# Decode attention with cached keys in SBUF: one slot of transposed K parked in two PSUM banks, a third V slot kept in SBUF

## The chip, the cores and the metric

The kernel runs on one NeuronCore of a Trainium2 chip. The metric is the device time of one execution in microseconds. Before the change it is 1142.0 us, the median of three runs (1141.01 to 1142.94). The profile shown was taken from one more execution of the same kernel, which took 1143.57 us; its span from the first to the last instruction is 1141.8 us.

## The reference

Two identical layers are applied one after the other to eight tokens (one per batch row). A layer is attention over a cache followed by a small dense block, each behind a layer norm without weights and a residual. Both layers read the same caches and the same weights.

```python
B, Sq, D = 8, 1, 512
Hq, Hkv, Sk, Dh = 32, 8, 8192, 128
# _A_ref(x, k_cache, v_cache, wq, wo):
q = (x @ wq).reshape(B, Sq, Hq, Dh).transpose(0, 2, 1, 3)
k = jnp.repeat(k_cache, 4, axis=1)
v = jnp.repeat(v_cache, 4, axis=1)
p = softmax(jnp.einsum("bhqd,bhkd->bhqk", q, k) * Dh ** -0.5)
o = jnp.einsum("bhqk,bhkd->bhqd", p, v)
... o (all heads) @ wo
# _B_ref(x, w1, w2):   silu(x @ w1) @ w2,  F = 1792
x = x + _A_ref(_layernorm(x), K, V, wq, wo)
x = x + _B_ref(_layernorm(x), w1, w2)
x = x + _A_ref(_layernorm(x), K, V, wq, wo)
x = x + _B_ref(_layernorm(x), w1, w2)
```

Everything is bfloat16. The two caches hold 134 MB each, far more than the on-chip memory, so most of them is read from HBM twice, once for each layer.

## The kernel before

**Tasks, chunks and slots.** A *task* is (layer, batch row b, K/V head g): 2 x 8 x 8 = 128 tasks. A task has four *chunks* k = 0..3 of 2048 cache rows. A chunk of K or of V is 512 KB and fills one of NSLOT = 28 *slots* of the SBUF tensor `arena`. Chunks are numbered c = 0..511 in the order of the tasks.

**What is done for a chunk.** The main loop (lines 946 to 987) runs over c. In iteration c it transposes K of chunk c on TensorE, eight 128x128 blocks into each of two PSUM banks (`emit_t`, line 520), ScalarE copies the first bank back over the first half of the slot (line 537) and VectorE the second (line 539); then `emit_pv` (line 608) multiplies the probabilities with V of chunk c-6 (LAG = 6), and `emit_s` (line 550) multiplies q with the transposed K of chunk c, into one of two score banks. Once per task come the row maximum (line 568), the exponential (line 581), the sums, and `emit_pt` (line 592), which transposes the probabilities P on TensorE into a bank of the same ring as K's transposes, from where VectorE copies them (line 601). This happens in iteration c = 4i+1 of the next task, between PV and the scores. A compute engine works strictly in the order in which the program emits its instructions.

**The ring.** The banks `TPp` are a ring of NTP = 3, counted by `evacs`: each half of a K chunk takes the next bank and each P transpose one more. PSUM has eight banks here: two for scores, `OTp` for the PV product, `UP`, three `TPp`, and `MISC` for the projections.

**What stays between the layers.** For each b the last KEEP = 20 of the 32 K chunks (heads 3 to 7) stay in SBUF, already transposed, from layer 0 to layer 1, and so do the last KEEPV = 2 V chunks. They are not loaded again in layer 1. `make_tasks` (line 137) orders the tasks so that for each b there is a run of five layer-0 tasks with g = 3..7 (I call it the *filling* run: each chunk loads K and V, K stays), then five or six tasks of other heads whose K and V stream through (the *streaming* run: 22 slots are held, six turn over), then five layer-1 tasks with g = 3..7 (the *emptying* run: no K load, no K transposes, V loads only, and each chunk gives a slot back).

**The loads.** `lay_loads` (line 193) writes the list of loads at build time. Positions are half-steps: 2c stands after PV of iteration c and 2c+1 after its scores. Every load has a position `need` at which it is used and a position `free` at which its slot is given back; it takes the slot that is free longest, and `after` is the position at which that slot was given back. Two loads of neighbouring chunks can be joined into one of 1 MB over two neighbouring slots (8 KB instead of 4 KB per partition, "wide"). SP issues all loads in the order of this list, each one behind a wait for the last reader of its slot. In the last three tasks K is transposed one chunk ahead (LEAD = 1, from chunk 500).

**The chain between the layers.** When a batch row has its eight layer-0 heads, `chain_of` (line 764) computes residual, layer norm, dense block, second norm and the new q in small steps put between the chunks. A projection of one token leaves its result in `MISC` in rows; `upright` (line 744) turns it with a VectorE 32x32-block transpose into `UP`, and the next operations read `UP`. There are five such turns for each b.

**Start.** The first AHEAD = 8 chunks of K are transposed, then `lay_runs` (line 489) brings eleven 512 KB runs of the weights into place through all eight PSUM banks, then q of layer 0 is projected when `wq` has landed.

Of the kernel before, what the change touches and what calls it, by code (L numbers as in the profile page):

```python
# [14 lines left out]
HALVES = 2  # L15
SPT = 4
NSLOT = 28
KEEP = 20
KEEPV = 2
LAG = 6  # L20
WIDE = 8
AHEAD = 8
LEAD = 1
NTP = 3
NSCP = 2
NQB = 2
NST = 4
KB = 512
# [141 lines left out]
    return 0 if (d.g, d.k) in kept else d.layer, d.b, d.g, d.k // 2  # L170


def plan_loads(tasks, kept, keptv, nslot, ngran):

    single = set()
    while True:
        loads = lay_loads(tasks, kept, keptv, nslot, ngran, single)
        double = {rows_of(d, kept) for d in loads if d.n == 2}
        torn = {rows_of(d, kept) for d in loads if d.n == 1} & double
        if not torn:  # L180
            return loads, double
        single |= torn


# [5 lines left out]
    return i * SPT  # L190


def lay_loads(tasks, kept, keptv, nslot, ngran, single):

    at = {t: i for i, t in enumerate(tasks)}
    wanted = []
    late = closing_from(tasks, kept)
    for i, (layer, b, g) in enumerate(tasks):
        for k in range(ngran):
            c = i * SPT + k  # L200
            if layer == 0 or (g, k) not in kept:
                last = i if layer or (g, k) not in kept else at[(1, b, g)]
                wanted.append(Load("K", layer, b, g, k, -1 if c < AHEAD else 2 * (c - LEAD if c >= late else c), 2 * (last * SPT + k) + 1))
            if layer == 0 or (g, k) not in keptv:
                last = i if layer or (g, k) not in keptv else at[(1, b, g)]
# [3 lines left out]
    loads = []  # L209
# [20 lines left out]
    return loads  # L230


def bass_interleave_layers__gqa_block_cached__dense_activation_silu__decode_kernel(
# [15 lines left out]
def _build(ctx, nc, A_x, A_k_cache, A_v_cache, A_wq, A_wo, B_w1, B_w2, out):  # L249
# [5 lines left out]
    KT = D // 128  # L255
# [12 lines left out]
    loads, wide = plan_loads(tasks, kept, keptv, NSLOT, NGRAN)  # L268
    NC = len(tasks) * SPT

    pe = nc.tensor
# [61 lines left out]
    last_use = [max(d.free for d in loads if d.slot <= s < d.slot + d.n) for s in range(NSLOT)]  # L333
    spare = last_use.index(min(last_use))

    def apart(space, shapes):
# [37 lines left out]
    def r_half(slot, h):  # L374
        return res(f"slot{slot}_{h}")
# [46 lines left out]
    with nc.Block() as block:  # L422

        @block.sync
        def _(sync_eng):
# [94 lines left out]
            def emit_t(c, h):  # L520
                if c >= NC:
                    return
                layer, b, g, k = where(c)
                if layer and (g, k) in kept:
                    return
                slot = k_slot[(b, g, k)]
                tb = evacs[0] % NTP
                evacs[0] += 1
                tpv = TPp[tb][:, :].rearrange("p (k q) -> p k q", q=128)
                steps = [  # L530
                    lambda c=c: pe.transpose(tpv[:, c, :], chunk(slot, h * GRP + c), ident[:, :])  # L531
                    for c in range(GRP)
                ]
                mm_group(steps, reads=[r_half(slot, h), "ident"], writes=[f"TP{tb}"])
                dst = half(slot, h)
                if h == 0:
                    op(act, lambda: act.copy(dst, TPp[tb][:, :]), reads=[f"TP{tb}"], writes=[r_half(slot, h)])  # L537
                else:
                    op(dve, lambda: dve.tensor_copy(dst, TPp[tb][:, :]), reads=[f"TP{tb}"], writes=[r_half(slot, h)])  # L539

            def emit_q(ti):
                layer, b, g = tasks[ti]
# [199 lines left out]
                return w.rearrange("p (c t b) -> p t c b", t=NT, b=QR)[:, :, c0:c1, :]  # L742

            def upright(n):
                op(dve, lambda: dve.transpose(UP[:, 0:n * QR], MISC[:, 0:n * QR]), reads=["MISC"], writes=["UP"])  # L745

            def sum_rows(xnew, rnew, xold, rold, by):
                upright(KT)
                op(dve, lambda: dve.scalar_tensor_tensor(
                    xnew, UP[:, 0:KT * QR:QR].unsqueeze(2), by, xold, op0=ALU.mult, op1=ALU.add),  # L750
                   reads=["UP", rold], writes=[rnew])

            def add_residual(xnew, rnew, xold, rold, n):
                op(
# [9 lines left out]
            def chain_of(b):  # L764
# [11 lines left out]
                hv = UP[:, 0:FT * QR:QR]  # L776

                def expo():
                    upright(FT)
                    op(act, lambda: act.activation(eh, hv, ACT.Tanh, scale=0.5), reads=["UP"], writes=["eh"])  # L780

                def silu():
                    op(dve, lambda: dve.scalar_tensor_tensor(hsT, eh, 1.0, hv, op0=ALU.add, op1=ALU.mult),
                       reads=["UP", "eh"], writes=["hsT"])

                def down(q0, q1):
                    def run():
# [12 lines left out]
                def answer(a):  # L800
                    def run():
                        upright(AC)
                        op(dve, lambda: dve.tensor_copy(qt2[:, a * AC:(a + 1) * AC], UP[:, 0:KB:QR]),
                           reads=["UP"], writes=[rq2])
                    return run

                n1, n2 = ln_stages(x1, "XT1", 1, one), ln_stages(x2, "XT2", 1, one)
# [138 lines left out]
            for c in range(NC + LAG):  # L946
# [81 lines left out]
```

## Time and profile before

| | |
|---|---|
| median of three runs | 1142.0 us |
| profiled execution | 1143.57 us, span 1141.8 us |
| TensorE busy | 937.2 us (82%), mean granted clock 0.917 |
| VectorE busy | 548.5 us (48%) |
| ScalarE busy | 482.9 us (42%) |
| DMA queue of SP | 456.71 MB, 99.3% of 16 engines |
| K and V loads | 283 of K and 363 of V, 202 of them 1 MB, the others 512 KB |

The profile is one execution. Its page gives busy times, the span in 40 slices, the DMA queues, and the chain of work that ended last (followed back from the last instruction to what released each step). Of the trace, groups of instructions, waits, stretches of time and single instructions can be asked for. Matmuls are pipelined, so a busy TensorE is not one at its peak. Times in the trace are in us from the start of the span, durations of single instructions are given in us or ns as marked.

### The profile page before, as it was taken

The page shows a single profiled execution, that of the slowest core. Times are in us where ns is not written, and L with a number is a line of the kernel's source. Part 1 is how long each engine was busy: PE and PEld are TensorE (multiplying, and loading weights), DVE is VectorE, ACT ScalarE, POOL GpSimd, SP SyncE. Part 2 cuts the span into 40 slices and gives each one's busy share as a digit, 9 for nine tenths or more (in the row PEclk, how much of TensorE's full clock was granted, in tenths as well). Part 3 has the DMA queues.
Part 4 walks back from the last instruction along what each step waited for, and adds up shares of the span by engine and source line. Part 5 has one row for each costly group of instructions (what it writes and reads, how often), then busy time and mean ns, then how long its engine had stood idle before and what let it go on. Part 6 is the DMA issues. An engine that isn't in the chain of part 4 may idle for free.

```text
span 1141.8 us, 42932 instructions
## 1 busy us (share of the span) xinstructions
PE 937.2 (82%) x18792; PEld 698.9 (61%) x18792; DVE 548.5 (48%) x1702; ACT 482.9 (42%) x770; POOL 117.4 (10%) x300
## 2 busy tenths in 40 slices
PE   7588888888888888888888887888788888888796
PEld 4366664666566665766566655666466655666565
DVE  7344553446434553446444553446444553446443
ACT  6254541554335441554235442554245432554332
POOL 0000101001110111001100011001100111001110
PEclk9698997999889996999889997999889997999887
DMA  9999999999999999999999999999999999999995
GB/s 378 413 414 414 395 403 413 419 411 397 412 418 417 394 404 419 419 405 396 414 418 415 392 404 418 418 401 398 413 417 403 391 395 420 417 389 392 396 420 225
DMA packets 96270, 459.45 MB, mean 402 GB/s; under 512 B 10700, under 2 KB 10964, under 8 KB 69716
## 3 DMA queue, kind: packets, MB, share of 16 engines
q1 hardware_dynamic: 96068, 456.71, 99.3%
q8 instruction: 148, 2.42, 0.9%
q14 instruction: 38, 0.31, 0.1%
q10 hardware_dynamic: 16, 0.01, 0.0%
HBM read 456.66 MB, written 0.01 MB: 400 GB/s over the span
## 4 chain that ended last, share of the span: by engine, by line
DMA 56%; PE 27%; DVE 9%; issue 4%; SPq 2%; ACT 0%; POOL 0%; POOLq 0%; ACTq 0%; DVEq 0%
DMA arena<-in_A_v_cache_dram 41%; PE TPp L531 14%; DMA arena<-in_A_k_cache_dram 12%; DVE arena L539 7%; PE SCp L557 6%; PE OTp L617 4%; DMA wq<-in_A_wq_dram 2%; PE MISC L732 2%; SPq L391 2%; PE TPp L597 1%; DVE small L606 0%; DVE small L587 0%; ACT P L581 0%; PE MISC L704 0%; DVE small L577 0%
## 5 line engine op out<-in xcount | busy, mean ns | idle before, releaser
L537 ACT COPY arena<-TPp 128x1024 bf16<-128x1024 bf16 x352 | 356.1, 1012 | 412.8 <-PE TPp L531 410.1
L539 DVE COPY arena<-TPp 128x1024 bf16<-128x1024 bf16 x352 | 243.4, 691 | 350.2 <-PE TPp L531 347.8
L531 PE MATMUL TPp<-ident,arena 128*128 128x128 bf16 x5632 | 389.4, 224 | 26.1 <-DMA arena<-in_A_k_cache_dram 23.4
L531 PEld LDWEIGHTS TPp<-ident,arena 128*128 128x128 bf16 x5632 | 328.2, 100 | 119.8 <-DMA arena<-in_A_k_cache_dram 66.8
L617 PE MATMUL OTp<-PT,arena 128*128 128x32 bf16 x8192 | 293.2, 179 | 74.2 <-DMA arena<-in_A_v_cache_dram 69.9
L617 PEld LDWEIGHTS OTp<-PT,arena 128*128 128x128 bf16 x8192 | 251.7, 98 | 159.6 <-DMA arena<-in_A_v_cache_dram 129.3
L557 PE MATMUL SCp<-arena,QB 128*32 128x512 bf16 x2048 | 223.8, 430 | 74.0 <-DVE arena L539 23.1
L581 ACT ACTIVATE P<-SCp,small 128x512 bf16<-128x512 f32 x128 | 87.9, 687 | 206.5 <-DVE small L579 139.8
L568 DVE TENSOR_REDUCE small<-SCp 128x1 f32<-128x512 f32 x128 | 88.5, 691 | 113.5 <-PE SCp L557 112.3
L557 PEld LDWEIGHTS SCp<-arena,QB 128*32 128x32 bf16 x2048 | 61.0, 96 | 115.2 <-ACT arena L537 62.1
L572 POOL PARTITION_ALL_REDUCE small<-small x128 | 47.5, 371 | 618.6 <-DVE small L570 618.6
L589 POOL PARTITION_ALL_REDUCE small<-small x128 | 55.2, 432 | 338.2 <-DVE at L631 155.1
L597 PE MATMUL TPp<-ident,P 128*128 128x128 bf16 x512 | 54.4, 235 | 9.6 <-ACT P L581 9.0
L587 DVE TENSOR_SCALAR small<-small 128x4 f32<-128x4 f32 x128 | 28.5, 223 | 37.9 <-ACT P L581 37.9
L601 DVE COPY PT<-TPp 128x256 bf16<-128x256 bf16 x128 | 36.6, 286 | 11.1 <-PE TPp L597 9.3
L597 PEld LDWEIGHTS TPp<-ident,P 128*128 128x128 bf16 x512 | 32.4, 102 | 12.8 <-ACT P L581 12.5
L570 DVE TENSOR_SCALAR small<-small 128x4 f32<-128x4 f32 x128 | 29.3, 229 | 4.5
L577 DVE TENSOR_TENSOR small<-small 128x4 f32<-128x4 f32 x128 | 19.9, 156 | 20.9 <-POOL small L572 20.9
L745 DVE STREAM_TRANSPOSE UP<-MISC 128x128 f32<-128x128 f32 (+2 forms) x40 | 22.1, 552 | 14.7 <-PE MISC L732 14.7
L732 PE MATMUL MISC<-wo,at 128*32 128x128 bf16 x1024 | 26.2, 232 | 0.0
L581 ACT ACTIVATION_READ_ACCUMULATOR P<-SCp,small 128x1 f32 x128 | 24.7, 193 | 0.0
L579 DVE TENSOR_REDUCE small<-small 128x1 f32<-128x4 f32 x128 | 20.1, 157 | 4.4
(96 smaller groups left out, 284.7 us busy)
## 6 DMA issues: line engine op xcount, KB each, us to landing
arena<-in_A_v_cache_dram SPq DMA_DIRECT2D x133, 1024.0 KB, 14.5
arena<-in_A_v_cache_dram SPq DMA_DIRECT2D x230, 512.0 KB, 6.6
arena<-in_A_k_cache_dram SPq DMA_DIRECT2D x214, 512.0 KB, 6.9
arena<-in_A_k_cache_dram SPq DMA_DIRECT2D x69, 1024.0 KB, 20.6
arena<-in_A_wo_dram SPq DMA_DIRECT2D x8, 512.0 KB, 13.9
wq<-in_A_wq_dram SPq DMA_DIRECT2D x1, 4096.0 KB, 25.1
w<-in_B_w_dram SPq DMA_DIRECT2D x1, 1792.0 KB, 22.3
arena<-in_B_w_dram SPq DMA_DIRECT2D x3, 512.0 KB, 17.1
```

The costliest lines, as they stand in the source:

```text
L531: lambda c=c: pe.transpose(tpv[:, c, :], chunk(slot, h * GRP + c), ident[:, :])
L537: op(act, lambda: act.copy(dst, TPp[tb][:, :]), reads=[f"TP{tb}"], writes=[r_half(slot, h)])
L539: op(dve, lambda: dve.tensor_copy(dst, TPp[tb][:, :]), reads=[f"TP{tb}"], writes=[r_half(slot, h)])
L557: lambda t=t: pe.matmul(SCp[bank][t * QR:(t + 1) * QR, :], QB[qn][:, NGRAN - 1 - k:NGRAN - 1 - k + QR], keys[:, t * KB:(t + 1) * KB], star ...
L568: op(dve, lambda: dve.tensor_reduce(mxp[st][:, :], SCp[bank][:, :], AX.X, ALU.max), reads=[f"SC{bank}"], writes=[f"mxp{st}"])
L572: op(pool, lambda: pool.partition_all_reduce(mxa[st][:, :], mxr[st][:, :], 128, bass.bass_isa.ReduceOp.max), reads=[f"mxr{st}"], writes=[f ...
L581: op(act, lambda: act.activation(P[:, :], SCp[bank][:, :], ACT.Exp, bias=nb[st][:, 0:1], scale=SM_SCALE, accum_out=rs[st][:, :]), reads=[f ...
L589: op(pool, lambda: pool.partition_all_reduce(ssa[st][:, :], ssm[st][:, :], 128, bass.bass_isa.ReduceOp.add), reads=[f"ssm{st}"], writes=[f ...
L597: lambda c=c: pe.transpose(tpv[:, c, :], P[:, c * 128:(c + 1) * 128], ident[:, :])
L601: op(dve, lambda: dve.tensor_copy(PT[:, :, :, :], tpv.rearrange("p c (t q) -> p c t q", q=QR)[:, :, :, 0:NGRAN * REP]), reads=[f"TP{tb}"], ...
L617: lambda n=n, cc=cc: pe.matmul(otp, chunk(slot, n), PT[:, cc % CPB, (cc // CPB) % NT, cc // (CPB * NT)::NGRAN].unsqueeze(2).to_broadcast([ ...
L732: lambda t=t, col=col, w=w, start=start, stop=stop: pe.matmul(MISC[t * QR:(t + 1) * QR, 0:math.prod(w.shape[1:])], spread(col), w, start=s ...
```

## The change

Three things change together.

1. *Parking.* Of the 20 kept K chunks of each b, the last one, (g, k) = (7, 3), no longer stays in SBUF. Its transposes of layer 0 go to two PSUM banks of their own, `KEPTp`, instead of ring banks. They are copied into the slot for the scores of layer 0 as before (`set_down`), then the slot is given back while the two banks keep their content. In layer 1, `emit_unpark` copies the two banks once more into a slot, by ScalarE and VectorE, one iteration before the scores need it. The slot comes from the planner, which picks the slot given back latest, but before position need - 1.
2. *A third V slot.* KEEPV goes from 2 to 3: V of (7, 1) now also stays between the layers and is not loaded in layer 1.
3. *The banks.* `UP` is dropped: VectorE turns `MISC` in place, and the operations that read `UP` read `MISC`. The ring of K's transposes goes from three banks to two. The weights at the start go through MISC in place of UP, and through the two ring and two KEPT banks.

```diff
-KEEPV = 2
+KEEPV = 3
+PARK = 1
...
-NTP = 3
+NTP = 2
...
-                last = i if layer or (g, k) not in kept else at[(1, b, g)]
+                last = i if layer or (g, k) not in kept - parked else at[(1, b, g)]
...
+            elif (g, k) in parked:
+                wanted.append(Load("C", layer, b, g, k, 2 * (c - 1), 2 * c + 1))
...
+        if d.kind == "C":
+            d.slot = max((j for j in range(nslot) if free[j] < d.need - 1), key=lambda j: (free[j], j))
+            free[d.slot] = d.free
+            copies.append(d)
+            continue
...
-    UP = ps_bank("UP")
     TPp = [ps_bank("TPp", BF16) for _ in range(NTP)]
     MISC = ps_bank("MISC")
+    assert PARK == 1
+    KEPTp = [ps_bank("KEPTp", BF16) for _ in range(HALVES)]
...
-                wide = [(SCp[0], "SC0"), (SCp[1], "SC1"), (OTp, "OT"), (UP, "UP")]
-                wide2 = [(TPp[n][:, :].bitcast(FP32), f"TP{n}") for n in range(NTP)] + [(MISC, "MISC")]
+                wide = [(SCp[0], "SC0"), (SCp[1], "SC1"), (OTp, "OT"), (MISC, "MISC")]
+                wide2 = [(p[n][:, :].bitcast(FP32), f"{r}{n}") for p, r in ((TPp, "TP"), (KEPTp, "KEPT")) for n in range(2)]
...
-                tb = evacs[0] % NTP
-                evacs[0] += 1
-                tpv = TPp[tb][:, :].rearrange("p (k q) -> p k q", q=128)
+                if (g, k) in parked:
+                    bank, rt = KEPTp[h], f"KEPT{h}"
+                else:
+                    tb = evacs[0] % NTP
+                    evacs[0] += 1
+                    bank, rt = TPp[tb], f"TP{tb}"
+                tpv = bank[:, :].rearrange("p (k q) -> p k q", q=128)
...
-                mm_group(steps, reads=[r_half(slot, h), "ident"], writes=[f"TP{tb}"])
+                mm_group(steps, reads=[r_half(slot, h), "ident"], writes=[rt])
+                set_down(bank, rt, slot, h)
+
+            def set_down(bank, rt, slot, h):
                 dst = half(slot, h)
                 if h == 0:
-                    op(act, lambda: act.copy(dst, TPp[tb][:, :]), reads=[f"TP{tb}"], writes=[r_half(slot, h)])
+                    op(act, lambda: act.copy(dst, bank[:, :]), reads=[rt], writes=[r_half(slot, h)])
                 else:
-                    op(dve, lambda: dve.tensor_copy(dst, TPp[tb][:, :]), reads=[f"TP{tb}"], writes=[r_half(slot, h)])
+                    op(dve, lambda: dve.tensor_copy(dst, bank[:, :]), reads=[rt], writes=[r_half(slot, h)])
+
+            def emit_unpark(d):
+                k_slot[(d.b, d.g, d.k)] = d.slot
+                for h in range(HALVES):
+                    set_down(KEPTp[h], f"KEPT{h}", d.slot, h)
...
-                op(dve, lambda: dve.transpose(UP[:, 0:n * QR], MISC[:, 0:n * QR]), reads=["MISC"], writes=["UP"])
+                op(dve, lambda: dve.transpose(MISC[:, 0:n * QR], MISC[:, 0:n * QR]), reads=["MISC"], writes=["MISC"])
...
-                        op(dve, lambda: dve.tensor_copy(qt2[:, a * AC:(a + 1) * AC], UP[:, 0:KB:QR]),
-                           reads=["UP"], writes=[rq2])
+                        op(dve, lambda: dve.tensor_copy(qt2[:, a * AC:(a + 1) * AC], MISC[:, 0:KB:QR]),
+                           reads=["MISC"], writes=[rq2])
...
                     emit_pv(c - LAG)
                     if (c - LAG) % SPT == SPT - 1:
                         emit_norm((c - LAG) // SPT)
+                while copies and copies[0].need <= 2 * c:
+                    emit_unpark(copies.pop(0))
                 issue_until(2 * c)
                 soft(c - SPT - 1, emit_pt)
```

More of the change, by code (lines that the diff above doesn't have):

```diff
@@ L170, in rows_of, with plan_loads @@
     return 0 if (d.g, d.k) in kept else d.layer, d.b, d.g, d.k // 2
-def plan_loads(tasks, kept, keptv, nslot, ngran):
+def plan_loads(tasks, kept, parked, keptv, nslot, ngran):
     single = set()
     while True:
-        loads = lay_loads(tasks, kept, keptv, nslot, ngran, single)
+        loads, copies = lay_loads(tasks, kept, parked, keptv, nslot, ngran, single)
         double = {rows_of(d, kept) for d in loads if d.n == 2}
@@ L180, in plan_loads @@
         if not torn:
-            return loads, double
+            return loads, copies, double
         single |= torn
@@ L190, in closing_from, with lay_loads @@
     return i * SPT
-def lay_loads(tasks, kept, keptv, nslot, ngran, single):
+def lay_loads(tasks, kept, parked, keptv, nslot, ngran, single):
     at = {t: i for i, t in enumerate(tasks)}
@@ L208, in lay_loads @@
     free = [-2] * nslot
-    loads = []
+    loads, copies = [], []
     while wanted:
         d = wanted.pop(0)
+        if d.kind == "C":
[3 more added lines that the diff above has]
+            continue
         mate = None
@@ L229, in lay_loads @@
         loads.append(d)
-    return loads
+    return loads, copies
 def bass_interleave_layers__gqa_block_cached__dense_activation_silu__decode_kernel(
@@ L267, in _build @@
     task_at = {t: i for i, t in enumerate(tasks)}
-    loads, wide = plan_loads(tasks, kept, keptv, NSLOT, NGRAN)
+    parked = set(order[len(order) - PARK:])
+    loads, copies, wide = plan_loads(tasks, kept, parked, keptv, NSLOT, NGRAN)
     NC = len(tasks) * SPT
@@ L332, in _build @@
     vr, yr, tr, s1, s1a = [few(B) for _ in range(5)]
-    last_use = [max(d.free for d in loads if d.slot <= s < d.slot + d.n) for s in range(NSLOT)]
+    last_use = [max(d.free for d in loads + copies if d.slot <= s < d.slot + d.n) for s in range(NSLOT)]
     spare = last_use.index(min(last_use))
@@ L749, in sum_rows @@
                 op(dve, lambda: dve.scalar_tensor_tensor(
-                    xnew, UP[:, 0:KT * QR:QR].unsqueeze(2), by, xold, op0=ALU.mult, op1=ALU.add),
-                   reads=["UP", rold], writes=[rnew])
+                    xnew, MISC[:, 0:KT * QR:QR].unsqueeze(2), by, xold, op0=ALU.mult, op1=ALU.add),
+                   reads=["MISC", rold], writes=[rnew])
             def add_residual(xnew, rnew, xold, rold, n):
@@ L774, in up @@
                            for k in range(KT) for t in range(NT)], ["w1", "xn1"])
-                hv = UP[:, 0:FT * QR:QR]
+                hv = MISC[:, 0:FT * QR:QR]
                 def expo():
                     upright(FT)
-                    op(act, lambda: act.activation(eh, hv, ACT.Tanh, scale=0.5), reads=["UP"], writes=["eh"])
+                    op(act, lambda: act.activation(eh, hv, ACT.Tanh, scale=0.5), reads=["MISC"], writes=["eh"])
                 def silu():
                     op(dve, lambda: dve.scalar_tensor_tensor(hsT, eh, 1.0, hv, op0=ALU.add, op1=ALU.mult),
-                       reads=["UP", "eh"], writes=["hsT"])
+                       reads=["MISC", "eh"], writes=["hsT"])
                 def down(q0, q1):
```

## The prediction

> **What bounds the kernel now.** I read the page first: the busy shares, the 40 slices with the DMA rows, the queue table and the head of the chain.
>
> ```profile
> span 1141.8 us, 42932 instructions
> PE 937.2 (82%) x18792; PEld 698.9 (61%) x18792; DVE 548.5 (48%) x1702; ACT 482.9 (42%) x770; POOL 117.4 (10%) x300
> ...
> DMA  9999999999999999999999999999999999999995
> GB/s 378 413 414 414 395 403 413 419 411 397 412 418 417 394 404 419 419 405 396 414 418 415 392 404 418 418 401 398 413 417 403 391 395 420 417 389 392 396 420 225
> ...
> q1 hardware_dynamic: 96068, 456.71, 99.3%
> ...
> DMA 56%; PE 27%; DVE 9%; issue 4%; SPq 2%; ACT 0%; POOL 0%; POOLq 0%; ACTq 0%; DVEq 0%
> ```
>
> The DMA engines are busy in every slice but the last; SP's queue alone takes 99.3% of them. TensorE, 82% by a modelled measure, is the largest share of the chain after DMA (27%). So the question is whether TensorE is ever the one that holds the end back. That needs the stretches. The next view gives busy times, clock, DMA share and rate for the end of one batch row's cycle: three tasks of an emptying run (from 303.3), its last task with the first filling one half begun (318.5), one filling task (338.8), two streaming tasks (384.9 and 395), and the time behind the last load.
>
> ```profile
> 303.30:308.80 5.50, 4.30 (x86) 2.55 (x84) 1.94 (x9) 0.86 (x3) 0.80 (x2) 0.81 1.02 424
> 308.80:313.90 5.10, 4.85 (x88) 2.72 (x84) 2.02 (x9) 0.87 (x3) 0.80 (x2) 0.50 1.01 422
> 313.90:318.50 4.60, 4.02 (x92) 2.55 (x88) 2.02 (x9) 0.86 (x3) 0.80 (x2) 0.97 1.01 413
> 318.50:328.60 10.10, 6.49 (x137) 4.44 (x136) 3.44 (x13) 2.66 (x6) 1.17 (x3) 0.79 1.01 417
> 338.80:347.90 9.10, 7.41 (x152) 6.13 (x152) 4.39 (x13) 4.92 (x7) 0.80 (x2) 1.00 1.01 419
> 384.90:395.00 10.10, 8.61 (x180) 6.49 (x180) 5.54 (x18) 4.92 (x7) 1.60 (x4) 1.00 0.99 377
> 395.00:405.70 10.70, 9.35 (x224) 7.27 (x224) 6.56 (x22) 5.21 (x9) 0.81 (x2) 1.00 1.01 401
> 1131.40:1139.30 7.90, 4.69 (x148) 4.26 (x148) 3.42 (x19) 0.61 (x3) 0.41 (x1) 0.50 0.01 2
> ```
>
> The share (last number but one) is 0.99 to 1.02 in all of them, also in the filling task, where a chunk costs TensorE and VectorE a fixed 2.28 us, as the chain in order of time shows (start, duration, what):
>
> ```profile
> 311.49 16.13 DMA arena<-in_A_v_cache_dram
> ...
> 338.76 0.40 PE SCp L557 x4
> 339.16 1.01 PE TPp L531 x16
> 340.19 0.69 DVE arena L539
> ...
> 341.03 0.40 PE SCp L557 x4
> ```
>
> From one scores group to the next are 341.03 - 338.76 = 2.27 us, less than the 2 x 1.25 us that DMA needs for K and V of a chunk at 419 GB/s (524,288 B / 419 GB/s = 1.251 us each). There TensorE eats up a lead that DMA has built in the emptying run. The lead is real data in flight: a 1 MB load takes 14.5 to 20.6 us to land, six to eight times its own 2.5 us, and SP stands behind slots that PV has still to give back:
>
> ```profile
> arena<-in_A_v_cache_dram SPq DMA_DIRECT2D x133, 1024.0 KB, 14.5
> arena<-in_A_k_cache_dram SPq DMA_DIRECT2D x69, 1024.0 KB, 20.6
> ...
> SPq L86 <- PE OTp L617: 545.2, 275, 10.7
> ```
>
> So SP's wait isn't idle DMA. Every stretch is paid in DMA time, and what TensorE loses or gains inside a stretch is taken back where it next waits for a load, as in the 16.13 us at 311.49. The end is paid so too: behind the last load (1131.4) there are 8 us of fixed work.
>
> **The loads that go.** V of (7,1) isn't loaded in layer 1: one 512 KB chunk for each of eight rows b, 4.19 MB of 456.71. It was a narrow load: the planner joins pairs only where the layout of the rows allows it in both layers, and heads 7 were never joined. I followed the planner's arithmetic for both sets of constants (positions only, no times). Before, 646 loads bring 848 chunks, 202 of them wide; after, 641 bring 840, 199 wide. Three pairs fall apart, one each of K and V of layer 0 and V of layer 1, so six chunks change from wide to narrow. Prices: a narrow chunk where narrow ones stream takes 524,288 / 401 = 1.307 us, a wide one 1.251 us at 419. The sum is 8 x 1.307 - 6 x 0.056 = 10.46 - 0.34 = **10.1 us** less. Bounds, all eight at the best and the worst rate of the stretches: 8 x 1.237 = 9.9 us (424) and 8 x 1.391 = 11.1 us (377).
>
> The Trainium skill, "DMA: Bandwidth & Descriptors", Specifications, puts the HBM limit of a core at about 358 GB/s; by it the eight chunks would be an estimated 11.7 us. The rows of 401 to 424 GB/s do not agree, and the rows decide.
>
> **Slots.** Parking frees one slot and the third V takes it: 22 slots stay held between the layers, six turn over, in both plans. In the streaming runs the issued lead is 5 chunks before and after, and as many loads (104 and 104) have only 5 or 6 half-steps between release and use. In the emptying run the new plan runs thinner at first: 4 chunks at the lowest against 5, then 7 against 9 and 10 against 12 in the next two tasks, because joined loads need two neighbouring slots; by its end it is level (19 against 18). I take that at nothing, since four chunks are 5 us of DMA work; its price if not is the second rival.
>
> **The copies back.** Sixteen copies are added, per b one of 1.01 us on ScalarE and one of 0.69 us on VectorE (the timeline below), 8 x 1.01 = 8.1 and 8 x 0.69 = 5.5 us of engine time. They are emitted in the iteration before the last chunk of an emptying run. They wait for PV of the iteration before that, and the scores of the last chunk wait for them. Here is that place for b = 1 (last chunk's scores at 323.25):
>
> ```profile
> 322.02 0.62 PE L557 MATMUL SCp<-arena,QB 128*32 128x512 bf16 x4
> 322.71 0.51 PEld L617 LDWEIGHTS OTp<-PT,arena 128*128 128x128 bf16 x16 [0.57 <-DMA arena<-in_A_v_cache_dram]
> 322.71 0.61 PE L617 MATMUL OTp<-PT,arena 128*128 128x32 bf16 x16
> 323.25 0.62 PE L557 MATMUL SCp<-arena,QB 128*32 128x512 bf16 x4
> 325.19 1.07 PE L531 MATMUL TPp<-ident,arena 128*128 128x128 bf16 x16 [0.78 <-DMA arena<-in_A_k_cache_dram]
> 327.67 0.59 PE L617 MATMUL OTp<-PT,arena 128*128 128x32 bf16 x16 [1.41 <-DMA arena<-in_A_v_cache_dram]
> ```
>
> The slot is released by the PV that ends about when the scores at 322.02 begin; 1.01 us on, the copy is done at about 323.1, before 323.25. What is queued behind it on ScalarE (q of the next task, the next evacuation) needs the later transposes at 325.19, and those wait 0.78 us for a load. Without that cover the cost is at most 1.01 us for each b, 8.1 us. The cover is there, so I take 0. The SP queue isn't passed: the copies issue no DMA, and the next load into that slot comes a run later.
>
> **The ring of two.** Transposes of chunk c+1 come behind scores of chunk c in TensorE's order, and those scores already wait for both evacuations of chunk c. So K's own transposes find both banks empty. The exception is the P transpose: as third user it now takes the bank that ScalarE is emptying. One such place in a filling run, by instruction:
>
> ```profile
> 338.91 0.69 ACT L581 ACTIVATE P<-SCp,small 128x512 bf16<-128x512 f32 x1 [0.42 <-DVE small L579]
> 339.75 1.01 ACT L537 COPY arena<-TPp 128x1024 bf16<-128x1024 bf16 x1
> 340.19 0.69 DVE L539 COPY arena<-TPp 128x1024 bf16<-128x1024 bf16 x1 [1.32 <-PE TPp L531]
> 340.40 0.38 PE L597 MATMUL TPp<-ident,P 128*128 128x128 bf16 x4
> 341.00 0.28 DVE L601 COPY PT<-TPp 128x256 bf16<-128x256 bf16 x1
> 341.03 0.40 PE L557 MATMUL SCp<-arena,QB 128*32 128x512 bf16 x4 [0.25 <-DVE small L587]
> ```
>
> ScalarE ends at 340.76, so P's transposes start at about 340.82, 0.42 us late. Their four matmuls follow each other in about 0.23 us, so the scores start near 341.05, not 341.03, and VectorE's copy of P near 341.1; the bank is needed again 0.9 us later (0.40 scores, half of 1.01). Loss on TensorE: 0.02 to 0.04 us a task, and at most 0.42. There are 88 transposing tasks, so 88 x 0.04 = 3.5 us at the small price and 37 us at the large one, all of it on an engine that makes good each delay at its next wait for DMA. I take 0.
>
> **Turning in place.** 40 turns, 0.33 to 0.73 us each; a turn within one bank has no row, the nearest is the same operation between two banks. Between nothing and a second pass of the same length: 0 to 16 x 0.73 + 8 x 0.63 + 16 x 0.33 = 22 us of VectorE. The added wait is that the next projection must not write MISC before its readers are done:
>
> ```profile
> 153.80 0.73 DVE L745 STREAM_TRANSPOSE UP<-MISC 128x512 f32<-128x512 f32 x1 [0.39 <-PE MISC L732]
> 154.57 0.17 DVE L803 CAST QT<-UP 128x16 bf16<-128x16 f32 x1
> 155.92 0.40 PE L732 MATMUL MISC<-wq,tiny 128*32 128x512 bf16 x4
> ...
> L745 DVE STREAM_TRANSPOSE UP<-MISC 128x448 f32<-128x448 f32 x8 | 5.1, 633 | 0.0
> L745 DVE STREAM_TRANSPOSE UP<-MISC 128x128 f32<-128x128 f32 x16 | 5.3, 331 | 8.2 <-PE MISC L732 8.2
> ```
>
> The reader ends at 154.74 and the next write comes at 155.92: 1.2 us to spare. 0.
>
> **Start.** The ring of two slows the first 16 half chunks, which ScalarE's 1.01 us copies pace, by up to 8 x 0.4 = 3 us (an estimate from those rows). Behind them TensorE waits for a weight load: 0.
>
> ```profile
> 38.68 3.58 PE L704 MATMUL MISC<-PT,wq 128*128 128x8 bf16 x128 [8.90 <-DMA wq<-in_A_wq_dram]
> ```
>
> **Sum.** The profiled execution took 1143.57 us, 1.8 above its span and 1.6 above the median. From 1143.57 - 10.1 = 1133.5 it is 1131.9 against the median: forecast **1132.0 us**, its own range 1130 to 1134.
>
> **Rivals.**
>
> *The P transposes bind (slower).* The point is 340.40 above. If P's transposes waited out the full 0.42 us and the scores with them, and the slots came back late by as much, DMA would starve too. In the 40 filling tasks, with their 2.27 us rhythm, this gives 40 x 0.42 = 16.8 us, more than the 10.1: 1142.0 - 10.1 + 16.8 = 1148.7. It decides from 10.1 / 40 = 0.25 us a task on. Against it: P's transposes would be through at 341.05, and the scores start at 341.03 anyhow. "Trainium Kernel Development and Optimization", Best Practices, of the Trainium skill notes that consistent bubbles can mean PSUM ran out; the trace has no such bubble yet, and no run here shows two banks. Chance 0.07.
>
> *The thin lead costs DMA time.* If in the first task of each emptying run (5.6 us) the rate fell from 420 to the 377 of the worst stretch, the loss is 5.6 x 0.10 x 8 = 4.6 us: 1136.5. For it: the new plan's 4 chunks. Against it: rows of 413 to 424 in this run. Chance 0.11.
>
> *Nothing changes.* The chunk's time is spent waiting for slots instead: 1142. For it: SP's 545.2 us behind PV. Against it: shares of 1.01. Chance 0.03.
>
> *More than the bytes.* The streaming runs are where DMA gets only 377 to 401. If one of two such tasks per b (10.1 us) rose from 377 to 401, 8 x 10.1 x 0.06 = 4.8 us more go: 1127. Nothing in the plan speaks for it. Chance 0.05.
>
> **Numbers.** Forecast 0.74. The range is 1129.5 to 1138.0: it takes in the forecast's bounds and the thin lead, and leaves out most of the three others. 0.2% (2.3 us) is about what a measurement of this kernel can tell from no change. Faster: 0.74 + 0.11 + 0.05 = 0.90; same 0.03; slower 0.07.
>
> **What would show it.** SP's queue moves 452.5 MB at about 99% of the engines and ends 10 us sooner; 352 + 8 copies on each evacuating line, with no long wait of the scores for them; P's transposes start right behind ScalarE's copy and the rhythm of 2.27 us stays; the turns keep 0.33 to 0.73 us; the stretches keep their rates. The prediction is wrong if the DMA share falls under 0.98 in an emptying run, or if the rhythm grows by tenths.

## The result

The changed kernel takes 1140.64 us, the median of 22 runs, against 1146.10 us for 22 runs of the kernel before: a ratio of 0.9953, with a 95% interval of 0.9932 to 0.9974. That is 5.4 us less (3.0 to 7.8), where the forecast of 1132.0 against 1142.0 was 10 us less, a ratio of 0.9912. Single executions of both kernels spread over 11 to 15 us (1141.01 to 1152.05 before, 1132.42 to 1147.28 after), and the three runs that the prediction had lie at the low end of that, so about 4 us of the distance to 1132 belong to the reference. The rest, about half of the forecast gain, is missing. All comparisons below are ratios against runs of the kernel before on the same chip, with their 95% intervals, turned into us at 1143 us.

The page of the profiled execution after the change (1136.29 us, span 1134.5 us): busy times, the DMA rows of the 40 slices, SP's queue, and the chain by engine.

```profile
span 1134.5 us, 42794 instructions
PE 935.0 (82%) x18792; PEld 698.9 (62%) x18792; DVE 558.3 (49%) x1710; ACT 491.0 (43%) x778; POOL 117.3 (10%) x300
...
DMA  9999999999999999999999999999999999999995
GB/s 376 413 413 415 392 407 412 420 411 385 405 419 416 391 408 417 419 411 392 412 419 415 394 403 418 418 403 393 407 419 411 381 408 419 417 388 367 396 420 224
...
q1 hardware_dynamic: 95348, 452.51, 99.1%
...
DMA 40%; PE 37%; DVE 11%; ACT 5%; issue 5%; SPq 2%; POOL 0%; POOLq 0%; ACTq 0%; DVEq 0%
```

The bytes went as planned, 456.71 to 452.51 MB. The busy time of SP's queue fell by about what was forecast: 0.993 x 1141.8 = 1133.8 us before, 0.991 x 1134.5 = 1124.3 us after, 9.5 us less, give or take 1 us, since the shares are rounded. The span fell by 7.3 us in this execution, so the time in which SP's queue did not fill the engines grew from 8.0 to 10.2 us. The chain changed more than anything: DMA's share went from 56% to 40%, and TensorE, VectorE and ScalarE together from 36% to 53%. ScalarE, with 0% before, now holds 5%. The experiments below show how much of this can be taken as a sign of the loss: DMA's share can't, and ScalarE's marks the ring of two.

Where ScalarE comes in is the place that the prediction had looked at, P's transposes. The chain in order of time, one filling chunk with P's transposes after the change (start, duration, what):

```profile
338.44 0.40 PE SCp L579 x4
338.84 0.57 PE TPp L545 x8
...
339.43 1.02 ACT arena L554
...
340.49 0.40 PE TPp L619 x4
340.89 0.33 PE SCp L579 x4
341.22 1.01 PE TPp L545 x16
```

The chain leaves TensorE after the first half of the transposes, goes through ScalarE's copy, and comes back to P's transposes and the scores. Shown by instruction:

```profile
339.43 1.01 ACT L554 COPY arena<-TPp 128x1024 bf16<-128x1024 bf16 x1
...
339.87 0.69 DVE L556 COPY arena<-TPp 128x1024 bf16<-128x1024 bf16 x1 [1.32 <-PE TPp L545]
...
340.49 0.40 PE L619 MATMUL TPp<-ident,P 128*128 128x128 bf16 x4 [0.27 <-ACT arena L554]
...
340.82 0.40 PE L579 MATMUL SCp<-arena,QB 128*32 128x512 bf16 x4
```

From scores to scores are 340.82 - 338.44 = 2.38 us, where it was 341.03 - 338.76 = 2.27: **0.11 us** a task. In the view of waits (us in total, times, longest) P's transposes now wait for ScalarE's evacuation, which before they never did:

```profile
PE TPp L619 <- ACT arena L554: 14.6, 53, 0.6
```

The filling tasks last 9.21 us instead of 9.10 (first scores to first scores, by the start times in the two traces).

What DMA does meanwhile is seen in a streaming run, which follows each filling run. The view gives busy times, clock, DMA share and rate of its first tasks in the last such run (from first scores to first scores; the last two numbers are share and GB/s). Before:

```profile
1010.00:1019.60 9.60, 7.54 (x152) 6.15 (x152) 4.53 (x13) 5.25 (x8) 0.80 (x2) 1.00 1.02 401
1019.60:1029.90 10.30, 8.63 (x186) 6.52 (x184) 5.53 (x19) 4.60 (x7) 1.60 (x4) 1.00 0.95 348
1029.90:1040.40 10.50, 9.43 (x224) 7.12 (x224) 6.44 (x22) 5.17 (x9) 0.81 (x2) 1.00 1.01 380
```

After:

```profile
1002.90:1012.10 9.20, 7.50 (x148) 6.16 (x149) 4.48 (x13) 4.93 (x7) 0.80 (x2) 1.00 1.03 408
1012.10:1021.30 9.20, 7.98 (x180) 6.61 (x181) 5.54 (x19) 4.92 (x7) 1.60 (x4) 1.00 0.99 342
1021.30:1034.00 12.70, 10.68 (x220) 7.66 (x221) 6.35 (x22) 5.11 (x8) 0.81 (x2) 0.87 0.92 333
```

Before, TensorE met DMA in the first streaming task (9.60 us, longer than its own 9.10). After, its own rhythm of 9.2 us runs through two streaming tasks. In the second of them the rate is down to 342 GB/s, which is no new thing (348 before); in the third it is 333 GB/s at a share of 0.92 where it was 380 at 1.01, and that task takes 12.70 us for 10.50. My reading, which this view alone doesn't show, is that DMA is ahead in the first two tasks with nothing but the six turning slots to load into, and TensorE gives them back 1% later than it could. The share hides much of this: at 0.99 the rate was 377 GB/s in a stretch of before and 342 in this one.

### The profile page after: what moved, and what is told of

Its sections match the earlier page's. It is cut to its first block, busy times and chain, and to the rows that moved or that the text cites. A ratio compares the mean times of both kernels' runs of the same rounds, so it can differ in the third digit from the quotient of the medians.

```text
span 1134.5 us, 42794 instructions
## 1 busy us (share of the span) xinstructions
PE 935.0 (82%) x18792; PEld 698.9 (62%) x18792; DVE 558.3 (49%) x1710; ACT 491.0 (43%) x778; POOL 117.3 (10%) x300
## 3 DMA queue, kind: packets, MB, share of 16 engines
q1 hardware_dynamic: 95348, 452.51, 99.1%
## 4 chain that ended last, share of the span: by engine, by line
DMA 40%; PE 37%; DVE 11%; ACT 5%; issue 5%; SPq 2%; POOL 0%; POOLq 0%; ACTq 0%; DVEq 0%
DMA arena<-in_A_v_cache_dram 32%; PE TPp L545 18%; PE SCp L579 9%; DVE arena L556 9%; DMA arena<-in_A_k_cache_dram 7%; PE OTp L639 4%; ACT arena L554 4%; PE TPp L619 2%; DMA wq<-in_A_wq_dram 2%; SPq L401 2%; PE MISC L754 2%; ACT P L603 1%; PE KEPTp L545 1%; DVE small L628 1%; DVE small L599 0%
## 5 line engine op out<-in xcount | busy, mean ns | idle before, releaser
L554 ACT COPY arena<-TPp 128x1024 bf16<-128x1024 bf16 x344 | 348.1, 1012 | 393.1 <-PE TPp L545 389.7
L545 PE MATMUL TPp<-ident,arena 128*128 128x128 bf16 x5504 | 377.8, 223 | 28.1 <-DMA arena<-in_A_k_cache_dram 22.3
L556 DVE COPY arena<-TPp 128x1024 bf16<-128x1024 bf16 x344 | 238.0, 692 | 329.7 <-PE TPp L545 327.0
L545 PEld LDWEIGHTS TPp<-ident,arena 128*128 128x128 bf16 x5504 | 317.9, 100 | 118.1 <-issue 62.1
L767 DVE STREAM_TRANSPOSE MISC<-MISC 128x128 f32<-128x128 f32 (+2 forms) x40 | 22.1, 552 | 10.0 <-PE MISC L754 10.0
```

Of the source, the lines that this page charges most:

```text
L554: op(act, lambda: act.copy(dst, bank[:, :]), reads=[rt], writes=[r_half(slot, h)])
L556: op(dve, lambda: dve.tensor_copy(dst, bank[:, :]), reads=[rt], writes=[r_half(slot, h)])
```

## The experiments

Three theories were set against each other. *Bytes*: the prediction's, all is paid in DMA time, and the shortfall is spread. *Rhythm*: with the bytes gone, TensorE's 9.2 us a task is on the path, and the ring's 0.11 us counts. *Slots*: DMA that is ahead only waits for one of six slots, with or without a ring of two.

### The change again, P's transposes elsewhere, the ring alone, the bytes alone

The change again:

> The change as it is, again, beside the others on one chip. Three theories stand. Bytes: every stretch is paid in DMA time, the eight loads left out give 10 us, and what fell short is the spread between executions. Rhythm: in the filling runs TensorE's rhythm (9.10 us a task before, 9.21 in the trace of after) is on the path too, and 7 such tasks for each b lose 0.11 us each, 8 x 7 x 0.11 = 6 us of the 10. Slots: in the streaming runs six slots turn over, and DMA that is ahead of TensorE only waits for slots, whatever the ring does. Expected: bytes -10 us, rhythm -4 to -5 us, slots -4 to -6 us.

Measured: 0.9985 (0.9968 to 1.0001), that is -1.7 us. In this comparison the change was hardly faster at all, and all three theories missed. Its profiled execution (span 1142.1 us) has one streaming run, from 502.3 to 553.7, in which DMA's rate stays low from end to end (even stretches of 10 us):

```profile
500.00:510.00 10.00, 8.24 (x160) 6.71 (x161) 4.78 (x13) 4.93 (x7) 0.80 (x2) 1.00 1.00 363
510.00:520.00 10.00, 8.77 (x204) 7.42 (x202) 6.26 (x21) 5.47 (x8) 1.62 (x5) 1.00 0.92 314
520.00:530.00 10.00, 7.90 (x133) 5.43 (x130) 4.79 (x19) 3.96 (x7) 0.79 (x2) 0.83 0.97 364
530.00:540.00 10.00, 7.70 (x187) 5.86 (x183) 6.51 (x25) 4.43 (x7) 1.59 (x4) 1.00 0.97 370
540.00:550.00 10.00, 9.37 (x152) 6.51 (x152) 4.62 (x12) 4.23 (x7) 0.81 (x2) 0.83 0.99 374
550.00:560.00 10.00, 8.22 (x165) 5.12 (x164) 5.30 (x15) 2.68 (x6) 1.02 (x3) 0.88 1.00 371
```

It lasts 51.4 us, where the other five streaming runs of five tasks in this trace last 47.2 to 49.1. So the loss isn't a fixed toll on each b; in this trace some 3 us of it lie in one streaming run.

P's transposes in the score bank that the exponential has just read, which leaves the ring of two to K alone:

```diff
-                tb = evacs[0] % NTP
-                evacs[0] += 1
-                tpv = TPp[tb][:, 0:KB].rearrange("p (c q) -> p c q", q=128)
+                bank, rt = SCp[ti % NSCP][:, :].bitcast(BF16), f"SC{ti % NSCP}"
+                tpv = bank[:, 0:KB].rearrange("p (c q) -> p c q", q=128)
...
-                mm_group(steps, reads=["P", "ident"], writes=[f"TP{tb}"])
+                mm_group(steps, reads=["P", "ident"], writes=[rt])
```

> The change, but P's transposes go into the score bank that the exponential has just read, so the ring of two serves K alone and P waits for no evacuation. Bytes: as the change itself, within 1 us. Rhythm: a filling task is back at 9.10 us or less, and the time is about 5 us under the change's, -10 us against before. Slots: as the change itself, -4 to -6 us, though the filling tasks are shorter.

Measured: 0.9936 (0.9917 to 0.9954), -7.3 us; run again beside the next set, 0.9921 (0.9898 to 0.9943), -9.0 us. That is 5.6 us under the change, as the rhythm theory had it, though short of its -10 against before. The first interval lies wholly under that of the change on the same chip. The chain of the same place, in the first of the two:

```profile
337.76 0.40 PE SCp L579 x4
338.16 1.01 PE TPp L545 x16
...
339.20 0.69 DVE arena L556
...
340.04 0.40 PE SCp L579 x4
```

ScalarE is off the chain here and the step is 2.28 us again; filling tasks last 9.10 us. The second and third task of the last streaming run, in the same execution:

```profile
1013.80:1022.90 9.10, 7.89 (x184) 6.59 (x184) 5.45 (x20) 4.93 (x7) 1.60 (x4) 1.00 0.99 359
1022.90:1033.80 10.90, 9.44 (x220) 7.11 (x224) 6.31 (x22) 5.20 (x9) 0.81 (x2) 1.00 1.02 403
```

So a dip of the rate in the second streaming task is there without the loss too. What differs from the change is that the rate is back at 403 in the next task, where it was 333.

The traces also say where the time went, by the starts of the scores. The change (span 1142.1 us) is 9.4 us longer than this execution (1132.7): 7.2 of them in the eight streaming runs that lie between filling and emptying (411.9 us together, against 404.7), 0.8 in the filling runs (379.8 against 379.0), 1.0 in the emptying runs (247.5 against 246.5).

The kernel before with a ring of two, its third bank used only for the weights at the start:

```diff
-NTP = 3
+NTP = 2
...
     MISC = ps_bank("MISC")
+    TPx = ps_bank("TPx", BF16)
```

> The kernel before with a ring of two banks and nothing else changed (the third bank lies idle but for the weights at the start). Bytes: 0, since TensorE makes it good at its next wait for a load. Rhythm: filling tasks of 9.21 us and +2 to +6 us. Slots: 0 to +1 us.

Measured: 1.0005 (0.9990 to 1.0019), +0.6 us, with filling tasks of 9.21 us. Here the ring does slow TensorE and it costs next to nothing, as the prediction said. The rhythm theory missed its +2 to +6. The trace shows the delay and how it is made good: the eight filling runs last 384.5 us together, against 379.3 before, but the streaming runs 407.4 against 409.1 and the emptying runs 244.5 against 249.4. Its chain by engine has ScalarE too, with no loss:

```profile
DMA 49%; PE 32%; DVE 9%; ACT 4%; issue 4%; SPq 2%; POOL 0%; POOLq 0%; ACTq 0%; DVEq 0%
```

The kernel before with the bytes of the third V slot alone (a quarter of each row is still loaded, 1 KB of 4 KB, not a half as the expectation's wording could be read):

```diff
+        if (d.kind, d.layer, d.g, d.k) == ("V", 1, HKV - 1, 1):
+            assert d.n == 1
+            dst, src = dst[:, 0:KB], src[:, 0:KB]
         dma(sp, dst, src, slsem[d.slot],
```

> The kernel before with its own slots, ring and turns, but of V (7,1) in layer 1 only the first half of each partition's row (1 KB of 4 KB) is loaded, in every b; the rest of that slot holds what was there, so the output is not the reference's. 3/4 of 8 loads go: 3.1 MB. Bytes: 3/4 of 10.1 = -7.6 us. Rhythm: -6 to -7.6 us, since the rhythm stays at 9.10. Slots: -3 to -4 us.

Measured: 0.9947 (0.9925 to 0.9970), -6.1 us, and run again 0.9931 (0.9904 to 0.9958), -7.9 us. The calculated 7.6 us lie inside both intervals, with no slot more or less. That speaks against the slots theory as the cause of the loss, and agrees with the prediction's price of the bytes.

### Is it the ring, or only a longer task?

The base of the next three is the version with P in the score bank, run again beside them:

> The change with P's transposes in the score bank, again, as the base for the three runs beside it. Expected as before: -6 to -9 us against the kernel before, filling tasks of 9.10 us.

Its result, -9.0 us, was given above. Then the same time on TensorE without a ring or a wait: in one chunk of each transposing task two transposes are done twice.

```diff
-                    for c in range(GRP)
+                    for c in (list(range(GRP)) + ([0, 1] if (k, h) == (1, 1) else []))
```

> The base, but chunk k = 1 of each transposing task does two of its sixteen transposes twice (about 0.13 us of TensorE a task). No ring, no wait is added. Rhythm theory (what the ring costs is only the longer task of TensorE, wherever it comes from): filling tasks of about 9.22 us and 4 to 6 us slower than the base, like the change itself. Ring theory (P's late copy holds up PV and the slots): as the base within 1 us. Bytes theory: as the base.

Measured: 0.9988 (0.9966 to 1.0009), -1.4 us: 7.6 us slower than its base, more than the 4 to 6 expected, and as slow as the change in the set above. Its chain by engine, and that of the base below it (DMA's share is no mark of the loss: the first execution of the base, the one with -7.3 us, had 40%):

```profile
DMA 39%; PE 39%; DVE 14%; issue 4%; SPq 2%; ACT 1%; POOL 0%; POOLq 0%; ACTq 0%; DVEq 0%
```

```profile
DMA 44%; PE 36%; DVE 13%; issue 4%; SPq 2%; ACT 1%; POOL 0%; POOLq 0%; ACTq 0%; DVEq 0%
```

and the chunk in which the two extra transposes stand:

```profile
343.31 0.40 PE SCp L579 x4
343.71 1.12 PE TPp L545 x18
...
344.86 0.69 DVE arena L556
...
345.70 0.40 PE SCp L579 x4
```

The step is 2.39 us and the filling task 9.21 us, almost the very numbers of the change (2.38 and 9.21), with P's transposes free of any wait. So what costs is the longer task, not P's lateness as such. In the last streaming run the dip of the second task is deeper than in the first execution of the base (359), 328 GB/s at a share of 0.96, and the rate is back in the third:

```profile
1024.90:1034.10 9.20, 7.99 (x182) 6.69 (x183) 5.44 (x19) 4.93 (x7) 1.60 (x4) 1.00 0.96 328
1034.10:1045.40 11.30, 9.48 (x226) 7.30 (x226) 6.45 (x22) 5.22 (x9) 0.81 (x2) 1.00 1.03 405
```

The other way, two transposes less in that chunk (and so a part of the scores wrong):

```diff
-                    for c in range(GRP)
+                    for c in range(GRP - 2 if (k, h) == (1, 1) else GRP)
```

> The base, but chunk k = 1 of each transposing task leaves out two of its sixteen transposes (so the scores of 256 cache rows are wrong there). Filling tasks of about 8.97 us. Rhythm theory: 1 to 4 us faster than the base, since TensorE still holds back part of the 10 us. Slots theory (DMA that is ahead only waits for slots): as the base or slower.

Measured: 0.9913 (0.9884 to 0.9942), -9.9 us, 0.9 us under its base, each inside the other's interval. Filling tasks last 8.99 us. A faster TensorE brings nothing that can be told from no gain, and the 1 to 4 us of the rhythm theory are neither shown nor ruled out. On this evidence DMA is the bound again at 9.10 us, and the two bounds meet between 9.10 and 9.21 us a task.

Seven turning slots in place of the third V slot:

```diff
-KEEPV = 3
+KEEPV = 2
```

> The base, but with two kept V slots as in the kernel before (KEEPV = 2): the parked slot is not spent on V, so seven slots turn over in the streaming runs, and the bytes are those of the kernel before. Bytes theory: 0 against the kernel before (199 joined loads for 202 are +0.3 us). Slots theory: -3 to -6 us, with more than 400 GB/s all through the streaming runs. Rhythm theory: -1 to +1 us.

Measured: 0.9964 (0.9945 to 0.9983), -4.1 us with all the bytes of before. The rhythm theory had no place for this, the slots theory had. Both have a part: a seventh slot is worth about 4 us, and spending it on V, with TensorE at 9.10, 7 to 9. (This run differs from the kernel before in parking, P's bank and the turns as well, but its rhythm is the same 9.10 us, and in its trace the eight streaming runs last 405.2 us together against 409.1.) What is gone are the slow executions: the twelve runs lie between 1139.28 and 1141.02 us, where the kernel before on the same chip goes from 1139.30 to 1151.69. The fastest is no faster. The rate did not stay over 400 GB/s, as the slots theory had it; the slices of the page still go down to 390:

```profile
GB/s 373 414 413 415 398 405 409 419 412 395 409 419 416 403 395 417 418 411 396 410 419 416 390 410 419 418 408 397 410 417 413 393 401 418 416 404 399 408 418 217
```

### The loss rebuilt from two parts, and the parts that should be free

> The kernel before with three quarters of the eight V loads left out, again, as the base for the next run. Expected -6 us (the first time -6.1), filling tasks of 9.10 us.

Its result, -7.9 us, was given above. The same with the ring of two added (both diffs above, nothing of the change besides):

> The base with the ring of two as well: no parking, no copies back, no turn in place, the slot plan of the kernel before. Rhythm theory: the ring, which cost nothing where all bytes were loaded, now costs 3 to 6 us; -1 to -3 us against the kernel before. If the loss comes from parking, the copies or the thinner plan: as the base, -6 us.

Measured: 0.9972 (0.9953 to 0.9990), -3.2 us. The ring that cost 0.6 us on the full bytes costs 4.7 us on the smaller ones (7.9 less 3.2; the two intervals just touch, but -6 us lies outside that of the second). The chain by engine, first the bytes alone (the run beside it), then bytes and ring:

```profile
DMA 55%; PE 28%; DVE 10%; issue 4%; SPq 2%; ACT 0%; POOL 0%; POOLq 0%; ACTq 0%; DVEq 0%
```

```profile
DMA 42%; PE 37%; DVE 10%; ACT 5%; issue 4%; SPq 1%; POOL 0%; POOLq 0%; ACTq 0%; DVEq 0%
```

The share of DMA in the chain is no steady mark, since the bytes alone had 45% in their first execution. ScalarE's goes with the ring of two, 0% without and 5% with it, but the ring alone had 4% and lost nothing. So the loss is there again without parking, copies, in-place turns or the new slot plan, and it takes both: the ring and the smaller bytes.

The turns in place, alone on the kernel before (`UP` replaced by `MISC` in `upright` and in its readers, as in the change's diff):

> The kernel before with VectorE's turns in place in MISC and nothing else (UP only lies idle behind the start). Turns of 0.33, 0.63 and 0.73 us as before; 0 us by every theory, within 1.5 us.

Measured: 1.0010 (0.9987 to 1.0033), no difference that can be told from none. The turns last as long within one bank as between two. In the profile of the change:

```profile
L767 DVE STREAM_TRANSPOSE MISC<-MISC 128x512 f32<-128x512 f32 x16 | 11.7, 731 | 5.4 <-PE MISC L754 5.4
L767 DVE STREAM_TRANSPOSE MISC<-MISC 128x128 f32<-128x128 f32 x16 | 5.3, 332 | 4.6 <-PE MISC L754 4.6
L767 DVE STREAM_TRANSPOSE MISC<-MISC 128x448 f32<-128x448 f32 x8 | 5.1, 633 | 0.0
```

The copies back, left out of the version with P in the score bank:

```diff
                 k_slot[(d.b, d.g, d.k)] = d.slot
-                for h in range(HALVES):
-                    set_down(KEPTp[h], f"KEPT{h}", d.slot, h)
```

> The change with P's transposes in the score bank, without the sixteen copies back: the scores of (7, 3) in layer 1 read whatever the slot holds, so the output is not the reference's. If the copies are covered: -6 to -9 us against the kernel before, as with them. If they hold up the scores: 2 to 8 us better than that.

Measured: 0.9913 (0.9886 to 0.9940), -9.9 us, against -7.3 and -9.0 with the copies, both on other chips. The intervals overlap: without the copies it is 0.9 or 2.6 us less, and neither is clear of nothing. In the trace of the change one of them looks covered: it ends at 322.67 on VectorE, while TensorE waits for a load of V until 322.28, and the scores come right behind PV's issue.

```profile
321.15 1.01 ACT L554 COPY arena<-KEPTp 128x1024 bf16<-128x1024 bf16 x1
...
322.01 0.66 DVE L556 COPY arena<-KEPTp 128x1024 bf16<-128x1024 bf16 x1
...
322.28 0.57 PE L639 MATMUL OTp<-PT,arena 128*128 128x32 bf16 x16 [0.40 <-DMA arena<-in_A_v_cache_dram]
322.82 0.40 PE L579 MATMUL SCp<-arena,QB 128*32 128x512 bf16 x4
```

### The better version

P's transposes in the score bank make the change what it was reckoned to be: 0.9936 and 0.9921 of the kernel before, and on the one chip where both ran together, 0.9936 (0.9917 to 0.9954) against the change's 0.9985 (0.9968 to 1.0001), 5.6 us apart. No run here beats it clearly with the whole computation in it.

## Why the prediction was wrong

*Direction and bytes: right.* The kernel became faster. Eight loads left out were priced at 10.1 us. DMA's busy time fell by 9.5 us; three quarters of the bytes alone gave 6.1 and 7.9 us where the price says 7.6; with P out of the way, the whole change gave 7.3 and 9.0, somewhat under the price. The limit of 358 GB/s that the Trainium skill gives ("DMA: Bandwidth & Descriptors", Specifications), by which it would be an estimated 11.7 us, is passed again by the rows of after, up to 420 GB/s.

*Ring of two: wrong, and this is the step that failed,* twice over. The first fault is the size. I had P's transposes 0.42 us late, which they are (they start 2.05 us behind the chunk's scores for 1.64 before; 0.27 us of it show as a wait on TensorE's row), but then let their four matmuls pass in 0.23 us, though the row that I showed has 0.38 for the four. In the trace of after the scores start 0.33 us behind them (340.49 to 340.82). With 0.33 the prediction's own sum gives 340.82 + 0.33 = 341.15 against 341.03, so the bound "0.02 to 0.04 us a task" should have been 0.12; measured are 0.11.

The second fault is the larger one: "I take 0", because TensorE "makes good each delay at its next wait for DMA". That was true of the kernel before, where the ring alone costs 0.6 us. It wasn't true of the changed kernel: there the same ring costs most of what the bytes had gained. My account of it is that the change itself takes away the waits in which the delay was made good. A filling run and the two tasks behind it, seven for each b, are 8 x 7 x 0.11 = 6.2 us; the runs show 4.7 us (bytes with and without the ring), 5.6 us (the change and P elsewhere, one chip) and 7.6 us for the same rhythm made with extra transposes.

I had read the streaming tasks of before as waiting for DMA without asking how much of that wait was there. The first two of each streaming run last 19.29 us together in the trace of before (the mean of eight runs of 18.20 to 19.84, first scores to first scores; 19.44 without the first run, which has no slack), 1.1 to 1.24 us more than twice 9.10. The change takes 1.25 us of DMA out for each b. That uses up the slack, so that each 0.11 us can count; after the change the two last 18.63 us, twice 9.21 and a little. The run with fewer transposes fits this: a slack that is just used up leaves nothing to gain from a faster TensorE.

That the slack is the reason is argued from these sizes, not shown step by step. Nor do the traces show the 6.2 us as a toll of 0.11 us on each task: between the change and the version with P elsewhere (spans 9.4 us apart) the streaming runs hold 7.2 us and the filling runs 0.8, but between the bytes alone and bytes with the ring (spans 5.0 apart) the filling runs hold 7.3 (383.2 against 375.9), the streaming runs 1.6, and the emptying runs give 2.2 back. Where the loss lands stays open.

*The rival that P's transposes bind* named the right mechanism and priced it too high for its place (0.42 us in 40 tasks, 16.8 us) with a chance of 0.07. Its point of decision, 0.25 us a task for no gain at all, was set too high: 0.11 us took half of the forecast gain in the first comparison and most of it in the second, and with seven tasks for each b in place of five the same sum gives 10.1 / 56 = 0.18.

*The share as proof.* A DMA share of 0.99 to 1.02 in the stretches quoted was taken to say that every stretch is paid in DMA time. It was so by a small margin only: in a streaming run that I had not quoted, the kernel before already falls to 348 GB/s at 0.95. And a share near 1 says little of the rate: the stretches at 0.99 range from 342 to 377 GB/s.

*Slots.* That "the issued lead is 5 chunks before and after" was beside the point: a seventh slot is worth 4.1 us, so six cost something already. The thin start of the emptying runs has not shown itself as a cause: bytes and ring rebuild the loss on the old slot plan, and in the trace of after the eight emptying runs last 245.4 us together, against 249.4 before. Of their first tasks seven ran at 401 to 416 GB/s, and only the last (from 1064.45) fell, to 370 GB/s at a share of 0.97.

*The signs that were named.* Both came, by little: the share is under 0.98 in that one emptying task, and the rhythm grew by a tenth of a us. SP's bytes, the starts of P's transposes and the turns came as foreseen.

*Turns in place: right at 0. Start: right*, the first scores start at 44.1 us in the trace of after, at 43.9 before. *Copies back:* taken at 0; the runs give 0.9 or 2.6 us, not clear of 0.

*The reference.* Three runs gave 1142.0; 22 gave 1146.1. The absolute range stood on the former. With the measured ratio 1142.0 would have become 1136.6, inside the range and beside the 1136.5 of the rival of the thin lead. That would have been luck: the range was wide enough for it, and the cause was another.

## What to carry to other kernels

When a change takes work off the bound, price every side cost against the slack that is left after it, not against the slack of the profile before: 0.11 us a task was free before and took half of the gain or more after. Read that slack off the stretch in which the chain goes back to the bound (here 19.3 to 19.44 us against 18.2), and compare it with what the change removes (1.25). Here a short ring of buffers was harmless to the stream that it serves in turn, and held up the odd third user; give that one a buffer that is free at that moment, here the bank of scores just read.

## What was not expected of the hardware

A DMA stream with six slots to turn over can stay slow once its rate has fallen: after the dip to 342 GB/s the next task still had 333 and took 12.70 us, and in one execution the rate stayed between 314 and 374 GB/s for 60 us. In other executions it was back over 400 in the next task. That may be why the same kernel's executions spread over 15 us (1132.42 to 1147.28), and why the gain came out as 0.9953 in one comparison and 0.9985 in the other, with intervals that overlap. The run with seven slots, whose twelve executions lie within 1.7 us, speaks for it. VectorE's 32x32 turn within one PSUM bank takes 731, 332 and 633 ns, as between two banks.
